# Chunked attention and a token-mixing MLP on one core: q/k in 18-token runs, masked key copies, v by token pairs

## The chip, the cores and the metric

The kernel runs on one core of one Trainium2 chip. The metric is the device time of one execution in microseconds, median of several runs; lower is better. Before the change it is 124.71 us (three runs, 123.63 to 127.87).

## The reference, cut to what matters

```python
# q, k, v: (8, 8, 576, 64) f32: batch, head, token, head dimension
q_c, k_c, v_c = (x.reshape(8, 8, 9, 64, 64) for x in (q, k, v))   # 9 chunks of 64 tokens
scores = q_c @ k_c.transpose(0, 1, 2, 4, 3) / 8.0
attn = softmax(scores, axis=-1)
x = (attn @ v_c).reshape(8, 8, 576, 64).transpose(0, 2, 1, 3).reshape(8, 576, 512)
wq, wk = x @ w_q, x @ w_k                                         # (8, 576, 64)
mixed = (wq @ wk.transpose(0, 2, 1) / 8.0) @ x
out = maximum(mixed, 0) @ w_out                                   # (8, 576, 512) f32
```

Attention stays inside each chunk of 64 tokens, so it is 576 small independent problems. The mixing step has no softmax, so the kernel computes it as wq @ (wk^T @ x) and never forms the 576 x 576 matrix.

## The kernel before, in words

The work goes batch by batch, and every step of every batch is a word in one long list, `ORDER`, which the kernel walks through at the end. A word is a step, a batch, a part and, behind `@`, a PSUM bank; behind `:` stands the engine of a copy, A for ScalarE and D for VectorE. Each engine executes its own instructions strictly in the order of the list. Waits between engines come from the data: an instruction waits until what it reads is written and what it overwrites has been read. So the list sets the order of the work, and the data sets the waits.

The steps of a batch b, with the lines of the profile:

- `LDb.*` (L116, L122, L129): GpSimd issues DMAs that read f32 from DRAM and write f16 into SBUF. q and k go to `qk`, as two runs of 16 tokens per partition and a rest of 4 (`q0-1`, `q1-2`, `qt`; heads 0 to 3 on partitions 0 to 63, heads 4 to 7 on the others). v goes to `vt` token by token, so that one DMA packet carries one token of one head, 256 bytes read and 128 written. There are three `vt` buffers; the load of batch b waits until batch b-3 has been used. All loads share eight completion semaphores in turn, so a load is issued when the load eight places earlier has landed.
- `CLi` (L137, L140): VectorE clears a `vt` buffer once and writes columns of ones. In `vt` two heads stand side by side, one on partitions 0 to 63 and one on 64 to 127, with zeros elsewhere, so that one product handles two heads and the column of ones gives the sum of the exponentials.
- `TRb.x` (L180): VectorE transposes q and k in blocks of 32 x 32, taking two f16 as one f32. Three parts each for q (even x) and k (odd x).
- `SCb.u` (L189): scores on TensorE. Each head uses 32 rows of the array twice (even and odd elements of the head dimension); four heads work side by side. u = 0 and 1 are 64 products of 64 columns each, u = 2 is 16.
- `EXb.u` (L204): the exponential on ScalarE, PSUM to `est`.
- `PVb.u` (L219): attention times v, 12 products each. `RNb.u` (L231, L232): VectorE divides by the sums and writes `xn`.
- `XT`, `XE` (L246, L273 or L275): transpose x through PSUM and copy it back. `PJ`, `EP` (L263): wq and wk. `TL`, `DU`: small copies of them. `WT`, `EW` (L291): transpose wk. `GM`, `EG` (L309): wk^T x, once per batch. `MX`, `RL` (L325, L340, L342): mixed, with the relu. `OM`, `OE` (L362): the output product of 128 rows and its copy out of PSUM, 36 in all; the copies collect in the space of used `qk` tiles, and SyncE stores them (L378).

`WS` loads w_q and w_k from SyncE, `WC` casts them, `WO` loads w_out, `CZ` clears a helper tile `zz` and `wtl`. The first store has a hand-made dependency on the last load, so the stores begin when all loads are done. `copy(eng, ...)` is one helper for all copies, so L273 (ScalarE) and L275 (VectorE) stand for many steps; the profile tells them apart by the tiles.

Of the kernel before, what the change touches and what calls it, by code (L numbers as in the profile page):

```python
# [11 lines left out]
F32 = mybir.dt.float32  # L12
AF = mybir.ActivationFunctionType
# [4 lines left out]
WS LD0.q1-2 CL0 CL1 LD0.q0-1 TR0.0 CZ TR0.2 LD0.k1-2 LD0.k0-1 TR0.3 TR0.1 CL2 LD0.v0-4 LD0.qt LD0.kt LD1.q0-2 ID  # L18
LD1.k0-2 LD1.kt LD1.v0-4 LD1.qt LD2.kt LD2.k0-2 LD2.q0-2 LD2.qt WO LD3.k0-2 LD2.v0-2 LD2.v2-4 SC0.0@0 EX0.0 SC0.1@2
EX0.1 TR0.4 TR0.5 PV0.1@2 RN0.1 PV0.0@0 RN0.0 SC0.2@4 EX0.2 PV0.2@4 TR1.0 RN0.2 TR1.1 TR1.3 TR1.2 TR1.4 TR1.5 XT0.0@0  # L20
XT0.1@4 XE0.1:A WC XE0.0:A SC1.0@2 SC1.1@4 PJ0@0 EX1.0 EX1.1 EP0:A PV1.0@4 SC1.2@2 TL0:A WT0@0 EX1.2 EW0:A PV1.2@2
GM0@0 EG0:A PV1.1@6 LD3.q0-2 LD3.kt LD4.k0-2 LD3.qt LD3.v0-2 LD3.v2-4 LD4.q0-2 LD5.qt LD5.q0-2 LD4.kt LD5.k0-2 LD4.qt
# [5 lines left out]
SC3.1@2 RN3.0 TR4.1 EX3.1 SC3.2@4 GM2@0 EX3.2 EG2:A PV3.1@2 RN3.1 MX2.1@0 RL2.1:A PV3.2@4 MX2.3@6 RL2.3:A MX2.0@0
RL2.0:A XT3.0@2 MX2.2@6 OM6@3 RN3.2 TR4.0 XT3.1@4 SC4.0@0 RL2.2:A XE3.0:D TR5.2 XE3.1:D TR4.5 TR5.1 OM10@2 PJ3@4
LD4.v2-4 LD5.kt LD5.v0-2 LD6.qt LD6.q0-2 LD6.kt LD6.k0-2 LD5.v2-4 LD7.kt LD7.q0-2 LD7.qt LD6.v0-2 LD7.k0-2 LD6.v2-4  # L30
OM11@6 OM7@7 TR4.2 TR4.3 OE10:A EX4.0 EP3:A TR4.4 DU3:D TR5.3 TR5.0 SC4.1@4 PV4.0@0 OE11:A TL3:A OE6:A EX4.1 OE7:A
OM9@3 WT3@2 PV4.1@4 SC4.2@6 OE9:A EW3:A EX4.2 RN4.0 TR5.5 TR5.4 RN4.1 SC5.0@0 EX5.0 PV4.2@6 GM3@2 RN4.2 EG3:A SC5.2@4
EX5.2 MX3.1@2 RL3.1:A MX3.0@0 RL3.0:D MX3.3@4 RL3.3:A XT4.1@6 XT4.0@2 OM12@3 OM13@4 TR6.0 XE4.0:D TR6.5 OE12:D OE13:D
XE4.1:A PJ4@6 OM14@4 MX3.2@2 EP4:A TL4:A RL3.2:A OE14:A TR6.1 TR6.4 TR6.3 PV5.0@6 SC5.1@0 SC6.2@2 EX5.1 OM15@5 WT4@4
EX6.2 EW4:A RN5.0 TR7.5 TR6.2 PV5.1@0 PV5.2@2 GM4@4 RN5.1 RN5.2 DU4:A OE15:A EG4:A OM16@6 MX4.3@4 MX4.1@0 TR7.4
RL4.1:D TR7.2 XT5.0@7 RL4.3:A XE5.0:A OE16:A XT5.1@2 OM17@4 OE17:A SC6.0@0 MX4.0@6 MX4.2@4 RL4.0:A EX6.0 XE5.1:D TR7.0
RL4.2:D TR7.1 PJ5@2 SC7.2@4 SC6.1@6 PV6.0@0 EP5:A LD7.v2-4 LD7.v0-2 OM18@2 TL5:D WT5@3 EX6.1 DU5:A EW5:A EX7.2 RN6.0
PV6.2@6 PV6.1@0 GM5@3 SC7.0@4 EG5:A OE18:D RN6.2 RN6.1 MX5.0@2 EX7.0 RL5.0:A OM20@6 XT6.0@7 MX5.2@4 RL5.2:A MX5.3@2
RL5.3:A MX5.1@0 OE20:D TR7.3 RL5.1:D XE6.0:D OM19@6 SC7.1@4 XT6.1@0 EX7.1 OE19:A XE6.1:D OM24@7 OE24:D PV7.1@4 PV7.0@0
PV7.2@2 PJ6@6 EP6:A RN7.1 RN7.0 RN7.2 TL6:A OM21@4 OM23@5 WT6@0 OM25@1 XT7.0@2 XT7.1@6 OE23:A XE7.0:D EW6:A OE21:A  # L40
XE7.1:D DU6:D GM6@0 EG6:A OE25:A OM22@2 MX6.2@6 MX6.3@0 RL6.3:D RL6.2:A PJ7@4 OM30@3 MX6.1@0 MX6.0@6 EP7:A RL6.1:A
RL6.0:A TL7:D WT7@4 OM26@5 OE22:D EW7:D GM7@4 EG7:A DU7:D OE26:D OE30:A OM29@6 OM28@7 MX7.1@2 RL7.1:D MX7.0@4 RL7.0:A
OE28:A OE29:D OM27@0 OE27:A MX7.3@2 MX7.2@4 RL7.3:D RL7.2:A OM31@1 OE31:A OM32@2 OE32:A OM35@1 OE35:A OM34@2 OE34:A
OM33@1 OE33:A
# [4 lines left out]
def kernel(  # L49
# [23 lines left out]
    RUN = 16  # L73
# [9 lines left out]
    vt = [sb.tile([P, NG, VP], F16, name=f"vt{i}") for i in range(NVB)]  # L83
    qkT = [sb.tile([P, 2, NG * 32, 2], F16, name=f"qkT{i}") for i in range(2)]
# [20 lines left out]
    halves = [x.rearrange("b (f h) s d -> b f (h s) d", f=2) for x in (q, k, v)]  # L105
    lead = NG // 16 * 16 * CH

    def load(b, what):
        s = "qkv".index(what[0])
        part = what[1:]  # L110
        for f in range(2):
            src = halves[s][b, f]
            rows = slice(CH * f, CH * f + CH)
            if s == 2:
                lo, hi = (int(x) * NG // 4 for x in part.split("-"))
                d = nc.gpsimd.dma_start(  # L116
                    vt[b % NVB][rows, lo:hi, f * (D + 2) : f * (D + 2) + D],
                    src.rearrange("(c p) d -> p c d", p=CH)[:, lo:hi, :],
                )
            elif part != "t":  # L120
                lo, hi = (int(x) for x in part.split("-"))
                d = nc.gpsimd.dma_start(  # L122
                    qk[b // 2][rows, b % 2, s, RUN * lo : RUN * hi].rearrange(
                        "p (u r) d -> p u (r d)", r=RUN
                    ),
                    src[0:lead].rearrange("(u p r) d -> p u (r d)", p=CH, r=RUN)[:, lo:hi],
                )
            else:
                d = nc.gpsimd.dma_start(  # L129
                    qk[b // 2][rows, b % 2, s, 32:36].rearrange("p r d -> p (r d)"),  # L130
                    src[lead:].rearrange("(p r) d -> p (r d)", r=4),
                )
            loads.append(d)
# [34 lines left out]
    def tr(b, u, s):  # L168
        at = (slice(0, 16), slice(16, 32), slice(32, 36))[u]
        r = RUN if u < 2 else 4  # L170
        to = qkT[b % 2][:, s].bitcast(F32).rearrange("p n o -> p (n o)")[
            :, 32 * at.start : 32 * at.stop
        ]
        frm = qk[b // 2][:, b % 2, s, at].bitcast(F32)
        if s or u == 2:
            to = to.rearrange("p (x r) -> p r x", r=r)
        else:
            to = to.rearrange("p (c r w) -> p r c w", c=8, r=r)
            frm = frm.rearrange("p r (c w) -> p r c w", c=8)
        nc.vector.transpose(out=to, in_=frm)  # L180

    def sc(b, u, bank):
        for c in range(8 if u < 2 else 2):
            tok = slice(512 * u + CH * c, 512 * u + CH * c + CH)
            for e in range(2):
                for i in range(4):
                    half = CH * (i // 2)
                    rows = slice(32 * i, 32 * i + 32)
                    nc.tensor.matmul(  # L189
                        ps[half : half + CH, bank + i % 2, CH * c : CH * c + CH],  # L190
                        lhsT=qkT[b % 2][rows, 1, tok, e],
                        rhs=qkT[b % 2][rows, 0, tok, e],
                        start=(e == 0),
                        stop=(e == 1),
                    )

    def ex(b, u, bank):
        n = CH * (8 if u < 2 else 2)
        src = ps[:, bank : bank + 2, 0:n]
        dst = est[b % 2][u].rearrange("p i n c -> p i (n c)")  # L200
        if u < 2:
            src = src.rearrange("p i (n r w) -> p (i n) w r", r=RUN, w=CH // RUN)
            dst = dst.rearrange("p i (n w r) -> p (i n) w r", r=RUN, w=CH // RUN)
        nc.scalar.activation(dst, src, AF.Exp, scale=scale_attn)  # L204

# [182 lines left out]
    for word in ORDER:  # L388
# [103 lines left out]
```

## Time and profile before

| What | Value |
|---|---|
| median of the runs | 124.71 us |
| the profiled execution | 124.75 us, span 122.7 us |
| TensorE busy | 94.9 us, 77% of the span |
| VectorE busy | 86.4 us, 70% |
| ScalarE busy | 68.0 us, 55% |
| GpSimd busy (issuing loads) | 64.6 us, 53% |
| DMA packets of the loads' queue | 45,088, 14.69 MB written |
| stores | 16, issued from 94.15 us on |

The span is the time from the first to the last instruction of the profile; the execution's own time is 2.05 us longer. The page gives busy time per engine, a strip of 40 slices (one digit per slice, the busy share in tenths), a chain of waits that ended last, and the costliest groups of instructions. In a line of a group, "out<-in" names the tiles, then come the shapes, the count, the busy time in us, the mean of one in ns, and behind the bar the idle time before them with what ended it. PE is TensorE, DVE VectorE, ACT ScalarE, POOL GpSimd, SP SyncE.

### The profile page before, as it was taken

How to read it: one execution, taken by the hardware profiler on the slowest of the kernel's cores; microseconds unless marked ns; L12 is line 12 of the kernel's file. 1: busy time of each engine (PE TensorE's matmuls, PEld its weight loads, DVE VectorE, ACT ScalarE, POOL GpSimd, SP SyncE). 2: the span in 40 equal slices, each digit the busy share in tenths (PEclk: the TensorE clock that was granted, in tenths of full speed). 3: DMA queues.
4: the chain of work that ended last, by engine and by line, in shares of the span. 5: the costliest groups of instructions: out<-in, count | busy, mean ns of one | idle time of the engine just before them, and what ended most of it. 6: DMA issues, size and time to landing. Idle time of an engine off the chain costs nothing.

```text
span 122.7 us, 4593 instructions
## 1 busy us (share of the span) xinstructions
PE 94.9 (77%) x2000; PEld 60.1 (49%) x2000; DVE 86.4 (70%) x147; ACT 68.0 (55%) x111; POOL 64.6 (53%) x104
## 2 busy tenths in 40 slices
PE   0001476887798899979998889599959999999970
PEld 0001475745573566465655655266536565544320
DVE  5777679624896789789997865799388894763500
ACT  4000610783498736777297936479936725463860
POOL 6997189648864489748985992389300000000000
PEclk9999999999999999999999999999999999999997
DMA  2999999999999999999999999999992999949794
GB/s 32 175 197 160 176 208 164 158 206 162 171 187 162 191 202 156 166 198 205 169 158 118 156 181 175 160 97 161 159 125 39 405 410 405 409 168 407 310 382 174
DMA packets 48499, 24.67 MB, mean 201 GB/s; under 512 B 39776, under 2 KB 42336, under 8 KB 48480
## 3 DMA queue, kind: packets, MB, share of 16 engines
q0 software_dynamic: 45088, 14.69, 113.5%
q1 hardware_dynamic: 3392, 9.70, 20.3%
q8 instruction: 15, 0.25, 0.8%
q14 instruction: 4, 0.03, 0.1%
HBM read 29.62 MB, written 9.44 MB: 318 GB/s over the span
## 4 chain that ended last, share of the span: by engine, by line
PE 42%; DMA 25%; POOL 11%; DVE 7%; issue 7%; ACT 5%; DVEq 0%; ACTq 0%; POOLq 0%
PE pb L362 17%; DMA vt<-in_v_dram 13%; DMA qk<-in_q_dram 6%; DMA qk<-in_k_dram 6%; POOL vt L116 5%; PE pb L263 5%; PE pb L219 5%; POOL qk L122 4%; PE pb L189 4%; DVE qkT L180 4%; PE pb L309 4%; PE pb L246 4%; PE pb L325 2%; DVE xn L232 2%; ACT rmx L340 2%
## 5 line engine op out<-in xcount | busy, mean ns | idle before, releaser
L180 DVE STREAM_TRANSPOSE qkT<-qk 128x512 f32<-128x512 f32 (+1 forms) x48 | 31.4, 706 | 11.6 <-DMA qk<-in_q_dram 6.2
L362 PE MATMUL pb<-wout,rmx 128*128 128x512 f16 x144 | 35.7, 381 | 0.1
L204 ACT ACTIVATE est<-pb 128x1024 f16<-128x1024 f32 (+1 forms) x24 | 19.0, 810 | 17.5 <-PE pb L189 17.5
L116 POOL DMA_DIRECT2D vt<-in_v_dram x28 | 25.3, 919 | 4.3 <-PE pb L189 1.2
L189 PE MATMUL pb<-qkT 32*64 32x64 f16 x1152 | 15.2, 204 | 14.2 <-DVE qkT L180 13.0
L232 DVE TENSOR_TENSOR xn<-pb,rec 128x768 f16<-128x768 f32 x24 | 23.0, 958 | 0.8
L189 PEld LDWEIGHTS <-qkT 32*64 32x64 f16 x1152 | 12.9, 117 | 17.9 <-DVE qkT L180 14.5
L362 PEld LDWEIGHTS <-rmx 128*128 128x128 f16 x144 | 13.0, 103 | 13.9 <-issue 1.6
L340 ACT ACTIVATE rmx<-pb 128x576 f16<-128x576 f32 x24 | 14.9, 651 | 5.4 <-PE pb L325 5.4
L273 ACT COPY qk<-pb 128x512 f32<-128x512 f32 x25 | 14.4, 590 | 5.4 <-PE pb L362 5.2
L219 PE MATMUL pb<-vt,est 128*64 128x130 f16 x288 | 14.2, 247 | 3.8 <-DMA vt<-in_v_dram 2.2
L219 PEld LDWEIGHTS <-est 128*64 128x64 f16 x288 | 11.1, 124 | 5.8 <-ACT est L204 2.4
L122 POOL DMA_DIRECT2D qk<-in_q_dram x18 | 10.5, 593 | 6.4 <-DMA vt<-in_v_dram 4.6
L122 POOL DMA_DIRECT2D qk<-in_k_dram x18 | 10.5, 603 | 5.8 <-DMA vt<-in_v_dram 4.3
L246 PE MATMUL pb<-ident,xn 128*128 128x128 f16 x144 | 11.0, 230 | 2.3 <-DVE xn L232 1.7
L246 PEld LDWEIGHTS <-xn 128*128 128x128 f16 x144 | 9.3, 103 | 4.6 <-issue 1.8
L273 ACT COPY xT<-pb 128x1280 f16<-128x1280 f16 (+1 forms) x6 | 6.9, 1153 | 7.3 <-PE pb L246 7.3
L129 POOL DMA_DIRECT2D qk<-in_q_dram x16 | 8.9, 584 | 3.1 <-DMA qk<-in_k_dram 1.9
L263 PE MATMUL pb<-xT,wpj 128*128 128x512 f16 x64 | 10.1, 305 | 0.4 <-ACT xT L273 0.4
L129 POOL DMA_DIRECT2D qk<-in_k_dram x16 | 8.7, 550 | 2.4 <-DMA qk<-in_k_dram 1.5
L275 DVE COPY qk<-pb 128x512 f32<-128x512 f32 x11 | 7.4, 682 | 1.8 <-PE pb L362 1.7
L275 DVE COPY xT<-pb 128x1024 f16<-128x1024 f16 (+1 forms) x10 | 7.1, 720 | 2.1 <-PE pb L246 2.1
(35 smaller groups left out, 81.1 us busy)
## 6 DMA issues: line engine op xcount, KB each, us to landing
out_dram<-qk SPq DMA_DIRECT2D x10, 768.0 KB, 6.4
qk<-in_q_dram POOLq DMA_DIRECT2D x14, 256.0 KB, 6.5
qk<-in_k_dram POOLq DMA_DIRECT2D x14, 256.0 KB, 6.8
vt<-in_v_dram POOLq DMA_DIRECT2D x24, 144.0 KB, 7.4
out_dram<-qk SPq DMA_DIRECT2D x6, 256.0 KB, 2.4
vt<-in_v_dram POOLq DMA_DIRECT2D x4, 288.0 KB, 7.6
qk<-in_q_dram POOLq DMA_DIRECT2D x4, 128.0 KB, 3.8
qk<-in_k_dram POOLq DMA_DIRECT2D x4, 128.0 KB, 5.3
```

The lines of the kernel that those rows point to most:

```text
L116: d = nc.gpsimd.dma_start(vt[b % NVB][rows, lo:hi, f * (D + 2) : f * (D + 2) + D], src.rearrange("(c p) d -> p c d", p=CH)[:, lo:hi, :],)
L122: d = nc.gpsimd.dma_start(qk[b // 2][rows, b % 2, s, RUN * lo : RUN * hi].rearrange("p (u r) d -> p u (r d)", r=RUN), src[0:lead].rearrang ...
L129: d = nc.gpsimd.dma_start(qk[b // 2][rows, b % 2, s, 32:36].rearrange("p r d -> p (r d)"), src[lead:].rearrange("(p r) d -> p (r d)", r=4),)
L180: nc.vector.transpose(out=to, in_=frm)
L189: nc.tensor.matmul(ps[half : half + CH, bank + i % 2, CH * c : CH * c + CH], lhsT=qkT[b % 2][rows, 1, tok, e], rhs=qkT[b % 2][rows, 0, tok ...
L204: nc.scalar.activation(dst, src, AF.Exp, scale=scale_attn)
L219: nc.tensor.matmul(ps[CH * o : CH * o + CH, bank + m // 3, at : at + VP].rearrange("p (f d) -> p f d", f=2)[:, :, 0 : D + 1], lhsT=est[b % ...
L232: nc.vector.tensor_tensor(out=xn[b % 2][:, 6 * u : 6 * u + 6].rearrange("p (k n) (f d) -> p k (n f) d", k=2, f=2), in0=xv[:, :, :, 0:D], i ...
L246: nc.tensor.transpose(t16[:, at % 1024 : at % 1024 + P], xn[b % 2][:, n, :], ident[:])
L273: nc.scalar.copy(dst, src)
L340: nc.scalar.activation(dst, src, AF.Relu, scale=scale_moe)
L362: nc.tensor.matmul(ps[:, bank, :], lhsT=c.rearrange("p (t r) -> p r t", r=size)[:, r], rhs=wout[:, i, :], start=(i == 0), stop=(i == NI - 1),)
```

## The change

- q and k are loaded as two runs of 18 tokens per partition (`RUN = S // 32`), one DMA for each half (`q0`, `q1`, `k0`, `k1`), all 128 partitions in one DMA. The rest pieces are gone. There are 32 such DMAs for 68.
- `TR` transposes half a batch of q or k at once, 576 elements per partition, two parts for each instead of three. q goes to `qT` (two buffers), k to `kN` (one buffer for all batches).
- New step `MKb.x`: each half of `kN` is copied twice into `kT`, multiplied by a mask that keeps the rows of one of two heads. An engine is named for each of the 32 copies: 18 on VectorE, 14 on ScalarE.
- `SC` takes 64 rows for each product with the two masked copies side by side as 128 columns, so one product gives the scores of two heads: 576 products for 1152. `EX` reads and writes without the rearrangement.
- v is read by pairs of tokens: a packet reads 512 bytes and writes 256, into partitions 32 to 95 only. New step `CPb.x` (`pair`): the second token of each pair is copied on the chip to partitions 0 to 31 or 96 to 127. 28 copies on VectorE, 4 on ScalarE.
- The clears of two `vt` buffers go to ScalarE, as a copy of zeros; the ones come from a small tile.
- `WS` moves behind the first loads, and its transfers wait for the eighth one. `WO` and `WS` are split in two parts each. `ZZ` (a product of zeros with zeros, five times) is new in the list. The first store depends on the second last load, the second on the last.
- `ORDER` is new. By its words, VectorE has 4 `OE` (11 before) and 3 `RL` (8); ScalarE has 32 `OE` (25), 29 `RL` (24) and 9 `XE` (6).

```diff
 ORDER = """
-WS LD0.q1-2 CL0 CL1 LD0.q0-1 TR0.0 CZ TR0.2 LD0.k1-2 LD0.k0-1 TR0.3 TR0.1 CL2 LD0.v0-4 LD0.qt LD0.kt LD1.q0-2 ID
+LD0.k1 MM CZ LD0.q1 LD0.k0 LD0.q0 CL1:D TR0.3 TR0.2 MK0.2:D MK0.3:D TR0.1 MK0.1:D SC0.1@0 TR0.0 MK0.0:D CL0:A LD0.v1
+LD0.v0 LD1.k0 LD1.q1 LD1.v0 LD1.k1 LD1.q0 WS CP0.0:D CP0.2:D CP0.3:D CP0.1:D TR1.1 SC0.2@2 SC0.0@4 CL2:A EX0.1 EX0.0
...
+LD7.v0 LD7.q1 PJ4@0 EP4:A SC5.0@2 OM17@5 OM12@0 SC5.2@6 EX5.0 TL4:A OE13:A OE17:A EX5.2 WT4@1 EW4:A CP5.0:D CP5.1:D
...
     def load(b, what):
+        if what[0] == "v":
+            n = int(what[1:])
+            half = NG // 2
+            for f in range(2):
+                dst = vcols(b % NVB, (2 * D + 2) * f, 2 * D)[
+                    32 + 32 * f : 64 + 32 * f, half * n : half * n + half
+                ]
+                src = v[b, 4 * n + 2 * f : 4 * n + 2 * f + 2].rearrange(
+                    "h (c i e) d -> i (h c) (e d)", i=32, e=2
+                )
+                loads.append(nc.gpsimd.dma_start(dst, src))
+            return
+        s, g = "qk".index(what[0]), int(what[1:])
+        loads.append(
+            nc.gpsimd.dma_start(
+                qk[b // 2][:, b % 2, s, RUN * g : RUN * g + RUN].rearrange("p r d -> p (r d)"),
+                (q, k)[s][b].rearrange("(x g) (p r) d -> g x p (r d)", g=2, r=RUN)[g],
+            )
+        )
+
+    def pair(b, n, f, eng):
+        half = NG // 2
+        g = slice(half * n, half * n + half)
+        to, frm = (slice(0, 32), slice(32, 64)) if f == 0 else (slice(96, P), slice(64, 96))
+        copy(
+            eng,
+            vcols(b % NVB, D + f * (D + 2), D)[to, g],
+            vcols(b % NVB, VW * f, D)[frm, g],
+        )
+
+    def clear(i, eng):
...
+        if eng == "A":
+            nc.scalar.copy(z, zero)
+        else:
+            nc.vector.memset(z, 0.0)
+        copy(eng, one, ones[:, None, :].broadcast_to([P, NG, 2]))
...
+    def tr(b, g, s):
+        to = (kN if s else qT[b % 2])[:, g].bitcast(F32).rearrange("p n o -> p (n o)")
+        frm = qk[b // 2][:, b % 2, s, RUN * g : RUN * g + RUN].bitcast(F32)
+        if s:
+            to = to.rearrange("p (e x r) -> p r e x", e=2, r=RUN // 2)
+            frm = frm.rearrange("p (r e) x -> p r e x", e=2)
         else:
+            to = to.rearrange("p (x r) -> p r x", r=RUN)
         nc.vector.transpose(out=to, in_=frm)
 
+    def mk(b, g, f, eng):
+        dst = kT[b % 2][:, g, :, f].rearrange("p c (e i) o -> p c e (i o)", e=2)
+        frm = kN[:, g].rearrange("p (e c i) o -> p c e (i o)", e=2, c=NCH)
+        if eng == "A":
+            nc.scalar.activation(dst, frm, AF.Copy, scale=mask[:, f : f + 1])
+        else:
+            nc.vector.tensor_scalar(dst, frm, mask[:, f : f + 1], None, op0=ALU.mult)
+
     def sc(b, u, bank):
+        for i in range(8 if u < 2 else 2):
+            g, c = (u, i) if u < 2 else (i, NCH - 1)
             for e in range(2):
+                for t in range(2):
+                    rows = slice(CH * t, CH * t + CH)
                     nc.tensor.matmul(
+                        ps[:, bank + t, CH * i : CH * i + CH],
+                        lhsT=kT[b % 2][rows, g, c, :, :, e].rearrange("p f n -> p (f n)"),
+                        rhs=qT[b % 2][rows, g, CH * c : CH * c + CH, e],
...
-    for d, back in zip(stores, (1,)):
+    for d, back in zip(stores, (2, 1)):
```

More of the change, by code (lines that the diff above doesn't have):

```diff
@@ L17 @@
 ORDER = """
-WS LD0.q1-2 CL0 CL1 LD0.q0-1 TR0.0 CZ TR0.2 LD0.k1-2 LD0.k0-1 TR0.3 TR0.1 CL2 LD0.v0-4 LD0.qt LD0.kt LD1.q0-2 ID
[L19 to L22, printed above, removed]
@@ L28 @@
[L28 to L32, printed above, removed]
@@ L33 @@
[L33 to L42, printed above, removed]
@@ new lines @@
+XE0.1:A WC SC1.0@4 PJ0@6 EX1.0 EP0:A TL0:A ZZ@2 SC1.2@2 EX1.2 WT0@6 EW0:A SC1.1@2 EX1.1 ZZ@0 GM0@0 EG0:A TR2.3 DU0:D
+TR2.1 CP1.3:D CP1.2:D PV1.0@2 MK2.3:A RN1.0 MX0.1@0 MX0.0@6 RL0.1:A RL0.0:A PV1.1@4 RN1.1 MX0.2@0 RL0.2:A MX0.3@2
+RL0.3:A PV1.2@6 MK2.2:A RN1.2 MK2.1:D TR2.2 MK2.0:D TR2.0 XT1.0@4 XE1.0:A OM2@2 CP2.0:D CP2.1:D XT1.1@6 XE1.1:A LD3.v0
+LD3.q1 LD3.v1 LD4.k1 OM0@3 OE0:A SC2.1@4 EX2.1 PJ1@6 LD4.k0 LD4.v0 LD5.k1 LD4.q1 LD4.q0 LD5.q0 LD4.v1 LD5.k0 LD5.q1
+TR3.1 EP1:A SC2.2@0 SC2.0@4 TL1:A EX2.2 EX2.0 DU1:A OE2:A WT1@6 OM1@7 EW1:D MK3.1:D CP2.2:D CP2.3:D MK3.0:D TR3.0
@@ L45 @@
+OM31@3 OE33:A OE31:D OM35@2 OE35:A OM34@0 OE34:A
 """.split()
@@ L72 @@
     VP = 2 * (D + 2)
-    RUN = 16
+    VW = 3 * D + 2
+    RUN = S // 32
     NVB = 3
@@ L82 @@
     qk = [sb.tile([P, 2, 2, NG, D], F16, name=f"qk{i}") for i in range(B // 2)]
-    vt = [sb.tile([P, NG, VP], F16, name=f"vt{i}") for i in range(NVB)]
-    qkT = [sb.tile([P, 2, NG * 32, 2], F16, name=f"qkT{i}") for i in range(2)]
+    vt = [sb.tile([P, (NG + 1) * VW], F16, name=f"vt{i}") for i in range(NVB)]
+    qT = [sb.tile([P, 2, S, 2], F16, name=f"qT{i}") for i in range(2)]
+    kN = sb.tile([P, 2, S, 2], F16, name="kN")
+    kT = [sb.tile([P, 2, NCH, 2, CH, 2], F16, name=f"kT{i}") for i in range(2)]
+    mask = sb.tile([P, 2], F32, name="mask")
+    ones = sb.tile([P, 2], F16, name="ones")
     est = [
@@ L104, with vcols @@
     loads = []
-    halves = [x.rearrange("b (f h) s d -> b f (h s) d", f=2) for x in (q, k, v)]
-    lead = NG // 16 * 16 * CH
+    def vcols(i, at, n):
+        return vt[i][:, at : at + NG * VW].rearrange("p (g c) -> p g c", c=VW)[:, :, 0:n]
     def load(b, what):
[L109 to L118, printed above, removed]
-                )
[L120 to L133, printed above, removed]
@@ L157, in small_weights @@
             for f in range(2):
-                nc.sync.dma_start(
-                    wst[CH * f : CH * f + CH, :, n, :],
-                    w.rearrange("(f k d) j -> f d k j", f=2, d=CH)[f],
+                for t in range(2):
+                    d = nc.sync.dma_start(
+                        wst[CH * f : CH * f + CH, 2 * t : 2 * t + 2, n, :],
+                        w.rearrange("(t f g d) j -> f t d g j", f=2, t=2, d=CH)[f, t],
+                    )
+                tc.add_manual_dep(
+                    d.ins,
+                    loads[7].ins.name,
+                    mybir.DependencyInfo(
+                        mybir.DependencyClass.Sync, mybir.DependencyReason.DATA
+                    ),
                 )
@@ L198, in ex @@
         n = CH * (8 if u < 2 else 2)
[L199 to L204, printed above, removed]
+        nc.scalar.activation(
+            est[b % 2][u].rearrange("p i n c -> p i (n c)"),
+            ps[:, bank : bank + 2, 0:n],
+            AF.Exp,
+            scale=scale_attn,
+        )
     def chunks(n):
@@ L404 @@
         if kind == "CL":
-            clear(n)
+            clear(n, eng or "D")
         elif kind == "CZ":
             nc.vector.memset(zz[:].bitcast(F32), 0.0)
+            nc.vector.memset(ones[:], 0.0)
+            for f in range(2):
+                nc.vector.memset(ones[CH * f : CH * f + CH, f : f + 1], 1.0)
             for w in wtl:
@@ L419 @@
             tr(n, x // 2, x % 2)
+        elif kind == "MK":
+            mk(n, x // 2, x % 2, eng)
+        elif kind == "CP":
+            pair(n, x // 2, x % 2, eng)
+        elif kind == "MM":
+            nc.vector.memset(mask[:], 0.0)
+            for i in range(4):
+                nc.vector.memset(mask[32 * i : 32 * i + 32, i % 2 : i % 2 + 1], 1.0)
         elif kind == "SC":
```

89 lines of the change are left out of this document (44 added, 45 removed).

## The prediction

> **What bounds the kernel now.** I read the engine table first, then the chain that ended last, then the timeline. The page:
>
> ```profile
> PE 94.9 (77%) x2000; PEld 60.1 (49%) x2000; DVE 86.4 (70%) x147; ACT 68.0 (55%) x111; POOL 64.6 (53%) x104
> ACT  4000610783498736777297936479936725463860
> DMA  2999999999999999999999999999992999949794
> ```
>
> TensorE (PE) and VectorE (DVE) are the full engines, ScalarE (ACT) has room, and DMA is busy to the end: loads to about 92 us, then stores. The chain in order of time:
>
> ```profile
> 80.94 7.35 DMA qk<-in_k_dram
> ...
> 88.39 1.04 DVE qkT L180
> ...
> 110.25 0.67 PE pb L309 x12
> ...
> 118.90 0.58 ACT qk L273
> ```
>
> A key load sets the time until 88 us, then TensorE without a gap until 118.9. I use L309 (GM, one per batch) as milestones. By the timeline, GM0 to GM7 end at 31.7, 41.0, 54.7, 68.4, 81.3, 92.5, 105.5 and 110.9 us; 8.6 us later the last compute ends, 3.2 us after that the span (122.7; its execution took 124.75, the median of the runs shown is 124.71). Load waits between GM3 and GM5, by the timeline of DVE (idle time in brackets):
>
> ```profile
> 71.52 0.71 DVE L180 STREAM_TRANSPOSE qkT<-qk 128x512 f32<-128x512 f32 x1 [1.37 <-DMA qk<-in_q_dram]
> 75.63 2.17 DVE L180 STREAM_TRANSPOSE qkT<-qk 128x512 f32<-128x512 f32 x3 [1.40 <-DMA qk<-in_k_dram]
> 79.68 0.93 DVE L180 STREAM_TRANSPOSE qkT<-qk 128x128 f32<-128x128 f32 x2 [0.86 <-DMA qk<-in_k_dram]
> 88.39 1.04 DVE L180 STREAM_TRANSPOSE qkT<-qk 128x512 f32<-128x512 f32 x1 [1.96 <-DMA qk<-in_k_dram]
> ```
>
> Together 5.6 us: that is about all that faster loads can give back there.
>
> **Prices**, from the groups by form:
>
> ```profile
> L204 ACT ACTIVATE est<-pb 128x1024 f16<-128x1024 f32 x16 | 16.2, 1024 | 12.9 <-PE pb L189 12.9
> L340 ACT ACTIVATE rmx<-pb 128x576 f16<-128x576 f32 x24 | 14.9, 651 | 5.4 <-PE pb L325 5.4
> L273 ACT COPY qk<-pb 128x512 f32<-128x512 f32 x25 | 14.4, 590 | 5.4 <-PE pb L362 5.2
> L273 ACT COPY wq<-wqk 64x576 f16<-64x576 f16 x4 | 2.7, 669 | 0.1
> L275 DVE COPY wq<-wqk 64x576 f16<-64x576 f16 x4 | 1.3, 327 | 0.8 <-ACT wqk L273 0.7
> ```
>
> The 64x64 copies (wtl) take 241 ns on ACT and 178 on DVE, so an SBUF element costs 0.84 ns on ACT and 0.29 on DVE. A masked key copy (MK) and a pair move (CP) have 1152 elements a partition: 1.15 us on ACT, 0.49 on DVE.
>
> **The change, part by part.**
>
> *Loads.* Counting the trace's DMA packets: 128-byte v packets pass at 2315 per 2 us (13.8 ns each on 16 engines), the 2048-byte q/k ones at 196 (163 ns). A line through both gives 23.7 ns for a v packet of 256 bytes (estimate; between 20.4 by bytes and 27.6, twice the old one) and 183 for a 2304-byte one. All loads: before 82.8 us, after 77.7 (bounds 74 to 82). POOL issues 68 loads for 98; issuing is hidden behind the packets themselves. The stores start with the second last load instead of the last; the final store follows the last OE in both. The last loads queue behind LD7.v1, which waits for PV4 to release its buffer near 80 us, so they land near 86; TR7.2, which needs the last, comes behind PV6 near 100. So the 5.6 us of waits go. If v packets gain nothing, the last lands near 90, still in time.
>
> *Transposes.* 48 become 32, each 576 elements. The old q form writes runs of four and takes 0.70 us, the k form writes strided and takes 1.04, the 128-element form, strided too, 0.394: 1.68 ns an element. Both new forms are strided: 1.15 us (0.79 if like the fast form, the low end). 36.8 us for 34.1.
>
> *Masked copies and pair moves.* 32 MK (18 on DVE, 14 on ACT) and 32 CP (28 and 4). DVE 46 x 0.49 = 22.5, ACT 18 x 1.15 = 20.7. tensor_scalar with a pointer from SBUF isn't in the trace: on DVE between 0.49 (the copy row) and 1.37 (one element a cycle, as in the fast transpose); I take 0.49, as the operands are f16 as in that row. MK on ACT reads its scale by pointer, which no row shows. The Trainium skill (ScalarE: Activation LUTs, What ACT_TABLE_LOAD costs) gives about 93 ns more for each such operand; by it the sum would be 1.3 us longer.
>
> *Moved to ACT.* Seven more OE (25 to 32, 4.1 us), five RL (24 to 29, 3.3), net three XE (2.8), and two clears: 2 x 2.4 us by the slope, hidden in the start, where ACT waited 10.9 us for its first score; without that cover they cost 4.8. Later DVE drops two clears (4.4), seven OE, five RL. Adding each list, less 0.045 us per instruction (before: ACT rows sum to 73.0, busy 68.0, 111 instructions): ACT 66.8 to 101.2, DVE 88.5 to 98.6.
>
> *Scores.* 1152 products become 576 of twice the width. Old: 64 take 0.64 us in the chain. New 32: between 0.48 (if two row halves run together, as the L325 pairs start together) and 0.96 (L291 transposes, the same 64x128 form, one in 0.030). I take 0.70, no change; the ends are 4 us either way in all. PE 84.2 to 85.5, with five ZZ.
>
> *Start.* By packet prices LD1.q0 lands at 20.6 (16.8 us of loads after a start of 3.8). Then TR1.0, SC1.0, EX1.0 to 23.7, PJ0 at the cold price of 2.08, EP0, WT0, EW0, GM0: end near 28.6 for 31.7 (bounds 27 and 31.7). CP0 waits for v0 (13.1) on DVE with TR1.1 and RN0 queued behind it, so PV0 starts near 15.1 (before 15.5). The weights wait on SP behind the eighth load, land near 18, and WC needs them near 22: covered. Early products are slow: 64 of L189 take 1.07 at 22 us, 0.70 at 35. The Trainium skill (TensorE: Matmul & The Clock Gate, Part 1) says that the clock rises after about 3.4 us of sustained work; the ZZ make that likelier, and by it the start would lose PJ0's 2.08 for 1.14, SC1.0's 1.07 for 0.70 and GM0's 1.32 for 0.74, 1.9 us. As TensorE is idle between these groups, I take none.
>
> *Sum.* I cut both order lists at the GM and add the prices, PE/DVE/ACT. Before: 7.3/8.9/7.3, 11.6/13.3/9.0, 12.4/13.2/10.3, 9.6/9.2/6.8, 9.2/8.3/8.7, 12.8/12.3/7.0, 5.5/1.8/3.3; the largest of each add to 72.5, measured 79.2, less 5.6 of load waits 73.6: a factor of 1.02. After: 9.2/15.1/11.9, 11.8/9.8/14.7, 9.2/14.4/12.7, 9.7/9.5/11.8, 11.0/9.9/11.6, 12.7/13.6/12.2, 6.5/3.0/5.4: 87.7 by stage, 81.4 by two stages (DVE and ACT lead in turn and may run ahead). Middle 84.5, times 1.02 is 86.2. So GM7 ends at 28.6 + 86.2 = 114.8, plus 8.6 and 3.2: span 126.6, plus 2.05: **128.6 us**. ACT, at 80% of its span, is the new bound. One more wait: kN is a single buffer, so a key transpose waits for the two MK before it, some on the full ACT queue, with RN and CP queued behind on DVE; I leave it in the factor.
>
> **Rivals.**
>
> *A, ScalarE packs (faster).* In a full ACT queue neighbours overlap more: two OE take 1.08 for 1.18, two RL 1.19 for 1.30, some 0.10 each. If ACT always has the next operand ready, its 80.3 us from GM0 to GM7 shrink by 97 x 0.055 to 75: GM7 at 103.6 to 107 with up to 4% of gaps, us 117.5 to 121. It decides once ACT's gaps stay below 4%. For it: bursts of three RL (1.74). Against: of 111 old instructions most didn't pack, and DVE, with 75 us there, must keep pace.
>
> *B, a swap.* The two-stage bound holds without the factor (81.4): us 123.8. For it: start and waits give 3.1 and 5.6 back. Against: between GM0 and GM3 the old stages took their largest sum or a little more.
>
> *C, no fast mode in the 46 DVE moves:* 0.88 more each, 40 us on DVE: about 160. Against: the 0.327 row.
>
> *D, the v part doesn't do what it says:* a packet of twice the bytes takes twice as long (27.6 ns), so CP is pure cost. Three v halves are ahead of LD1.q0, 1152 packets and 0.28 us each, so the start is 0.8 later: 129.4. Against: 4 KB packets pass more bytes per ns than short ones. The Trainium skill (DMA: Bandwidth & Descriptors, Specifications) puts full rate at transfers of 512 bytes and up, which the new writes of 256 still miss; that speaks for D.
>
> **How the numbers follow.** Forecast 0.46 (own range 125.5 to 133), A 0.24, B 0.19, C 0.05, D 0.06. Faster by over 2% (under 122.2; 2% is about what a measurement of this kernel can tell from no change): A and a little of B, 0.27. Within: most of B and the forecast's edge, 0.20. Slower (over 127.2): 0.53. The range leaves out the end of A, C and the tail: 119 to 137.
>
> **What would show it.** Right: ACT busy near 100 us, DVE 95 to 100, no DMA wait of L206 transposes past 30 us, GM0 near 28.6, GM stages with ACT or DVE full. Wrong: transposes near 0.8, MK or CP on DVE near 1.3, ACT below 90, or PE waits on loads past 60 us.

## The result, and the profile after

The changed kernel takes 142.46 us (median) against 125.13 for the kernel before in the same comparison: ratio 1.133, 95% interval 1.101 to 1.165, clearly slower. The forecast was 128.6, its range 119 to 137. Some executions of one and the same kernel are longer than its others by one to four per cent; the ratio, and every difference in time below, leaves them out, and then the changed kernel takes 140.7 us (140.00 and 141.36) and the kernel before 124.2. The profiled execution took 140.0 us with a span of 138.2.

The page of the changed kernel: the engine table, then strips of 40 slices of 3.5 us each.

```profile
PE 96.2 (70%) x1429; PEld 58.3 (42%) x1429; DVE 99.7 (72%) x160; ACT 101.2 (73%) x151; POOL 47.5 (34%) x74
...
ACT  7900033384459999999999798599999999786640
...
GB/s 13 44 160 182 175 153 123 141 161 144 126 137 163 163 151 163 169 152 132 176 137 135 147 174 154 166 184 153 163 103 236 265 418 411 405 143 153 290 274 199
```

The engines hold the work that was forecast (VectorE 99.7 us for 98.6, ScalarE 101.2 for 101.2), and yet the span is 11.6 us longer than the forecast span of 126.6. ScalarE's strip hints where: it is full only from the thirteenth slice on, at 41 us. The milestones (end of GM, L344 now) by the timeline:

| | GM0 | GM0 to GM7 | GM7 to the end of the span | span |
|---|---|---|---|---|
| before | 31.7 | 79.2 | 11.8 | 122.7 |
| forecast | 28.6 | 86.2 | 11.8 | 126.6 |
| after | 42.2 | 84.9 | 11.1 | 138.2 |

The start holds the whole miss: GM0 ends 13.6 us later than forecast. Its timeline, first VectorE, then ScalarE (idle time and what ended it in brackets):

```profile
12.60 1.20 DVE L206 STREAM_TRANSPOSE kN<-qk 128x576 f32<-128x576 f32 x1 [7.72 <-DMA qk<-in_k_dram]
```

```profile
36.25 0.62 ACT L194 CAST wpj<-rmx 128x512 f16<-128x512 f32 x1 [3.49 <-DMA rmx<-in_moe_w_k_dram]
```

and the chain that ended last, in order of time:

```profile
6.49 12.29 DMA vt<-in_v_dram
22.69 13.46 DMA rmx<-in_moe_w_k_dram
36.92 2.12 PE pb L298 x8
```

The first key load was issued at 1.26 us and its transpose began at 12.60. The small weights, held behind the eighth load, were issued from 18.8 us on, the last piece of w_k at about 22.7, and landed at 36.15. The cast WC stands on ScalarE ahead of EX1.0, and PJ0 on TensorE waits for it. "Land near 18" was wrong by 18 us, and with it "covered". Every load is slow, not the first alone (DMA issues: count, KB, median us to landing; before, q and k took 6.5 and 6.8):

```profile
qk<-in_k_dram POOLq DMA_DIRECT2D x16, 288.0 KB, 11.1
qk<-in_q_dram POOLq DMA_DIRECT2D x16, 288.0 KB, 10.9
vt<-in_v_dram POOLq DMA_DIRECT2D x32, 144.0 KB, 10.8
```

The packets tell why. The row of the loads' queue (packets, MB, their time as a share of 16 engines' span):

```profile
q0 software_dynamic: 36416, 14.73, 113.4%
```

Of these packets the trace counts 13,376 of 4 bytes, before 1,568. Before, that is 16 for each of 98 loads. After, 68 loads x 16 = 1,088 leave 12,288, which is 384 for each of the 32 q/k loads. A q/k load has 128 data packets. If four engines carry them, each has 32, and 12 idle engines with as many 4-byte packets each make 12 x 32 = 384. From 5 us on the 2304-byte packets landed per us climb 19, 34, 44, 68, 87 as loads are added; four engines at 183 ns pass 22, sixteen pass 87. The trace does not name the engine of a packet, but both counts fit a q/k load that runs on 4 of 16 (theory T1). What changed is the shape of its read: `"(x g) (p r) d -> g x p (r d)"` takes every second head, four stretches of 32 runs with a gap between, so the slowest dimension counts 4. In the kernel before it counted 64. The Trainium skill (DMA: Bandwidth & Descriptors, Why a DMA increments its semaphore by 16 and not by 1) states this rule: the largest number up to 16 that divides the slowest dimension of both sides is the number of engines. The counts agree. I priced the packets and did not look at the outer dimension.

Rival theories: T2, the weights' new place in the queue is the cause by itself; T3, the added copies on VectorE and ScalarE are.

### The profile page after: what moved, and what is told of

Its sections match the earlier page's. It is cut to its first block, busy times and chain, and to the rows that moved or that the text cites. A ratio compares the mean times of both kernels' runs of the same rounds, so it can differ in the third digit from the quotient of the medians.

```text
span 138.2 us, 3452 instructions
## 1 busy us (share of the span) xinstructions
PE 96.2 (70%) x1429; PEld 58.3 (42%) x1429; DVE 99.7 (72%) x160; ACT 101.2 (73%) x151; POOL 47.5 (34%) x74
## 4 chain that ended last, share of the span: by engine, by line
DMA 36%; PE 27%; ACT 20%; DVE 6%; issue 3%; SPq 3%; POOL 1%; ACTq 0%; DVEq 0%
DMA vt<-in_v_dram 16%; PE pb L397 12%; DMA qk<-in_q_dram 10%; DMA rmx<-in_moe_w_k_dram 10%; ACT est L232 5%; PE pb L298 4%; PE pb L281 4%; DVE xn L267 4%; ACT rmx L375 3%; PE pb L222 3%; ACT qk L308 3%; SPq L181 3%; ACT kT L212 2%; PE pb L360 2%; DVE qT L206 2%
## 5 line engine op out<-in xcount | busy, mean ns | idle before, releaser
L222 PE MATMUL pb<-qT,kT 64*128 64x64 f16 x576 | 13.5, 200 | 22.7 <-DVE kT L214 18.2
L129 POOL DMA_DIRECT2D vt<-in_v_dram x32 | 21.6, 677 | 20.3 <-DMA qk<-in_q_dram 5.7
L206 DVE STREAM_TRANSPOSE kN<-qk 128x576 f32<-128x576 f32 x16 | 19.4, 1215 | 11.5 <-DMA qk<-in_k_dram 11.3
L222 PEld LDWEIGHTS <-kT 64*128 64x128 f16 x576 | 11.4, 101 | 28.6 <-DVE kT L214 18.3
L206 DVE STREAM_TRANSPOSE qT<-qk 128x576 f32<-128x576 f32 x16 | 19.6, 1242 | 4.6 <-DMA qk<-in_q_dram 4.6
L212 ACT ACTIVATE kT<-kN,mask 128x1152 f16<-128x1152 f16 x14 | 17.5, 1265 | 3.0 <-DVE rec L264 2.8
L133 POOL DMA_DIRECT2D qk<-in_q_dram x16 | 11.7, 731 | 13.1 <-DMA vt<-in_v_dram 6.1
L133 POOL DMA_DIRECT2D qk<-in_k_dram x16 | 11.3, 707 | 12.1 <-DMA qk<-in_k_dram 6.6
L310 DVE COPY vt<-vt 32x1152 f16<-32x1152 f16 x28 | 12.4, 458 | 1.0 <-DMA vt<-in_v_dram 0.3
L360 PE MATMUL pb<-wqk,g 64*128 64x288 f16 x32 | 7.1, 290 | 5.3 <-DVE xn L267 2.3
L308 ACT COPY xT<-pb 128x1024 f16<-128x1024 f16 (+1 forms) x9 | 9.6, 1095 | 0.0
(44 smaller groups left out, 95.3 us busy)
## 6 DMA issues: line engine op xcount, KB each, us to landing
qk<-in_k_dram POOLq DMA_DIRECT2D x16, 288.0 KB, 11.1
```

What stands on the lines that cost most here:

```text
L129: loads.append(nc.gpsimd.dma_start(dst, src))
L133: nc.gpsimd.dma_start(qk[b // 2][:, b % 2, s, RUN * g : RUN * g + RUN].rearrange("p r d -> p (r d)"), (q, k)[s][b].rearrange("(x g) (p r) ...
L212: nc.scalar.activation(dst, frm, AF.Copy, scale=mask[:, f : f + 1])
L222: nc.tensor.matmul(ps[:, bank + t, CH * i : CH * i + CH], lhsT=kT[b % 2][rows, g, c, :, :, e].rearrange("p f n -> p (f n)"), rhs=qT[b % 2] ...
L308: nc.scalar.copy(dst, src)
```

## The experiments

**One stretch per q/k load (e1_all_engines).** The heads are dealt out so that a load reads four neighbouring heads; v then needs one load per head, and the weight rows follow. With more v loads, the load that the small weights wait for is the twelfth and no longer the eighth; it is the same one, the last of `LD0.v0`.

```diff
-                (q, k)[s][b].rearrange("(x g) (p r) d -> g x p (r d)", g=2, r=RUN)[g],
+                (q, k)[s][b].rearrange("(g x) (p r) d -> g (x p) (r d)", g=2, r=RUN)[g],
...
-                src = v[b, 4 * n + 2 * f : 4 * n + 2 * f + 2].rearrange(
-                    "h (c i e) d -> i (h c) (e d)", i=32, e=2
-                )
+                for h in range(2):
+                    src = v[b, 4 * h + 2 * n + f].rearrange("(c i e) d -> i c (e d)", i=32, e=2)
...
-                        moe_w_out.rearrange("(t f g p) m -> f t p g m", f=2, t=2, p=CH)[f, t],
+                        moe_w_out.rearrange("(g t f p) m -> f t p g m", f=2, t=2, p=CH)[f, t],
...
-                    loads[7].ins.name,
+                    loads[11].ins.name,
```

> The changed kernel with its head order altered: partition quarter x of half g holds head 4g + x instead of 2x + g, so that a q/k load reads one unbroken stretch of 128 runs and not four stretches of 32; v is then loaded per head (64 loads of v instead of 32) and the weight rows follow. Bytes, packets (128 of 2304 B for each q/k load) and all compute stay. T1 (the four stretches of a q/k load put it on 4 of the 16 DMA engines, so its 128 packets take 32 x 183 ns = 5.9 us in a row instead of 8 x 183 ns = 1.5 us): the first load lands at about 6.5 to 8 us and not 12.5, w_k lands by 28 and not 36, the first GM ends at 28 to 32 and not 42.2, and the time is 42.2 - 30 = 12 us less, 125 to 131 us; the 4-byte packets of the q/k queue fall from 13,376 to some 1,600. T2 (the small weights, issued only behind the eighth load, set the start by themselves): the first GM ends at 38 or later and the time is 136 or more. T3 (the added masked copies on VectorE and ScalarE set the start): the first GM ends within 3 us of 42.2, time 137 to 142.

126.92 us, ratio to the kernel before 1.017 (1.005 to 1.028): 14.0 us less than the changed kernel (126.7 for 140.7). The 4-byte packets are 1,600 = 100 loads x 16. The row of the loads' queue, VectorE's first transpose, and the strip of GB/s:

```profile
q0 software_dynamic: 24640, 14.69, 84.8%
```

```profile
5.39 1.22 DVE L208 STREAM_TRANSPOSE kN<-qk 128x576 f32<-128x576 f32 x1 [0.51 <-DMA qk<-in_k_dram]
```

```profile
GB/s 24 183 197 172 188 187 207 192 189 181 187 145 196 168 160 175 189 203 193 173 137 131 204 188 210 183 115 122 302 410 408 404 191 204 134 5 245 257 318 188
```

The first transpose starts at 5.39 for 12.60; the second slice moves 183 GB/s for 44. GM0 ends at 33.4 (forecast of T1: 28 to 32, missed by 1.4), GM0 to GM7 takes 81.1 us for 84.9. T1 holds; T3 can have little of it. w_k still lands at 26.3 and the cast still waits 3.0 us.

**v per head alone (e10_v_per_head_only)**, the control for the other half of that edit.

```diff
-                src = v[b, 4 * n + 2 * f : 4 * n + 2 * f + 2].rearrange(
-                    "h (c i e) d -> i (h c) (e d)", i=32, e=2
-                )
+                for h in range(2):
+                    src = v[b, 4 * n + 2 * f + h].rearrange("(c i e) d -> i c (e d)", i=32, e=2)
...
-                    loads[7].ins.name,
+                    loads[11].ins.name,
```

> Control for the one-stretch run, which changed the v loads as well: the changed kernel with v loaded per head (64 loads of 72 KB instead of 32 of 144 KB), its q/k loads left in four stretches. T1 (the q/k pattern alone made the difference): no gain; 32 x 0.6 us more for issues on GpSimd and the same q/k loads: 140 to 148 us, first GM at 41 to 44. T7 (smaller v loads, which free the window of loads in flight sooner, are part of the gain): first GM at 39 or earlier, 130 to 138 us.

162.99 us: not a gain but 19 us more (159.5 for 140.7), beyond what I expected of T1 too. VectorE's waits (us in total, times, longest):

```profile
DVE kN L208 <- DMA qk<-in_k_dram: 20.3, 8, 7.0
DVE qT L208 <- DMA qk<-in_q_dram: 17.8, 7, 4.7
```

So the v split alone brings no gain; with it in both runs the q/k pattern is worth 33 us, 159.5 to 126.7. What the split does to one-stretch loads no run shows, so the 14.0 us are the worth of both halves of the edit together. My reading is that eight loads are in flight at most, and four-engine loads need four of their kind among them to fill 16 engines; twice as many v loads leave fewer places. That is argued from the window of eight, not shown by a run.

**The weights first (e2_weights_first).** `WS` at the head of the list, without the dependency on the eighth load.

```diff
-LD0.k1 MM CZ LD0.q1 LD0.k0 LD0.q0 CL1:D ...
-LD0.v0 LD1.k0 LD1.q1 LD1.v0 LD1.k1 LD1.q0 WS CP0.0:D ...
+WS LD0.k1 MM CZ LD0.q1 LD0.k0 LD0.q0 CL1:D ...
+LD0.v0 LD1.k0 LD1.q1 LD1.v0 LD1.k1 LD1.q0 CP0.0:D ...
...
-                tc.add_manual_dep(d.ins, loads[7].ins.name, ...)
```

> The changed kernel with the small weights w_q and w_k issued first of all and without their wait for the eighth load; nothing else is changed. T1 (the q/k loads on 4 engines set the start; the weights are only one of the things that they delay): the cast of the weights no longer waits 3.5 us and the projection no longer 3.3 us, the first GM ends at about 39 and the time falls by some 3 us, to 136 to 140. T2 (the late weights are the whole loss): the first GM ends at 32 or earlier, time 127 to 132. T3 (the copies): first GM within 1.5 us of 42.2, time 140 to 143.

140.62 us. GM0 ends at 38.9 (for 42.2), as T1 said, and T2 falls. How much of the 3.3 us reaches the end stays open: three executions took 140.6 to 140.9 us and one took 137.8, which is 2.9 less than the changed kernel. In the profiled one, of 140.58 us, GM0 to GM7 takes 89.0 us for 84.9. VectorE's waits for loads in it:

```profile
DVE kN L199 <- DMA qk<-in_k_dram: 13.7, 7, 7.4
DVE qT L199 <- DMA qk<-in_q_dram: 5.7, 4, 2.8
DVE vt L303 <- DMA vt<-in_v_dram: 2.2, 3, 0.8
```

These are 21.6 us, in the changed kernel 16.2: in this execution what the weights give back is waited for later.

**Both (e3_engines_and_weights)**, the diffs of the one-stretch run and of the weights together.

> Both edits together: the changed kernel with the q/k loads in one stretch of 128 runs each, and the small weights issued first. T1 (the start was lost to loads on 4 engines, and behind them to the weights that queue after the eighth load): the cast of the weights and the projection behind it, which in the run with the one-stretch loads still waited 3.0 us for w_k landing at 26.3, wait for nothing; the first GM ends at 29 to 30.5 instead of 33.4, the rest stays (81 us to the last GM, 10.7 us behind it), so a span of 121 to 122.5 and a time of 122.5 to 124.5 us: 0 to 2% under the kernel before. T3 (the copies on VectorE and ScalarE are what is left of the start): first GM at 32 or later, time 126 or more.

125.22 us over 12 runs, ratio 0.998 (0.9935 to 1.0029): level with the kernel before. GM0 ends at 30.7; both figures lie just above T1's ranges (30.5 and 124.5), and below what T3 asked for. The weights are worth 1.5 us here (126.7 to 125.2). The two edits, one of layout and one of order, take back the whole loss: the ratio of 1.133 becomes 0.998.

**The engine count in another kernel.** The kernel before with its 16-token loads issued one unit at a time (control), and the same with the 64 runs of a load read as 4, 8 or 16 stretches. Only the pattern's order differs; the tokens come out permuted.

```diff
-                    src[0:lead].rearrange("(u p r) d -> p u (r d)", p=CH, r=RUN)[:, lo:hi],
+                    src[0:lead].rearrange("(u c a r) d -> u a c (r d)", c=CH // 4, a=4, r=RUN)[u],
```

> Control for the run with four stretches: the kernel before, with each q/k load issued per 16-token unit in two loads instead of one, its 64 runs read in their own order. All theories: within 2.5% of the kernel before (123 to 128 us); some 0.5 to 1 us more for the additional issues at the start, and 4-byte packets at 16 for each load.

> The kernel before, with each q/k load issued per 16-token unit and its 64 runs read as 4 stretches of 16 with a step between (the tails of 4 tokens likewise); the tokens land on other partitions, so the output is that of permuted tokens. Bytes, packets and compute are those of the kernel before. T1 (outermost count of 4 puts a load on 4 engines): packets of 4 B on the load queue rise from 1,568 by some 300 for each such load, the first loads take 16 packets in a row on each engine instead of 4 (some 2 us longer each), the first GM ends 4 to 12 us later than in its control, and the time is 130 to 140 us. T2 and T3 (it is the weights, or the copies, that cost the changed kernel its start; the pattern of the read does nothing): like its control within 1.5%, 123 to 127 us.

> The kernel before with the 64 runs of a q/k load read as 16 stretches of 4 with a step between (tails likewise; the output is that of permuted tokens). It tells the engine count from the broken order of the read. T1 (the number of engines is set by the outermost count, here 16): like the control, 131 to 134 us, some 2,000 packets of 4 B, first GM at 32 to 33. T4 (a read in stretches is slow in itself, whatever their number): like the run with four stretches, 145 or more.

> The same with 8 stretches of 8 runs. T1 (8 engines of 16): 8 packets in a row on each engine, 8 idle engines with as many 4-byte packets each, so 2,016 + 96 x 64 = 8,160 of them, and a time between the control's 132.6 and the four stretches' 154.5, nearer to the control since two loads in flight fill all engines: 134 to 143. T4: 145 or more.

| slowest dimension | time, us | ratio to before (interval) | 4-byte packets | first GM ends |
|---|---|---|---|---|
| 64 (control) | 132.61 | 1.062 (1.039 to 1.084) | 2,016 | 32.4 |
| 16 | 130.98 | 1.038 (1.030 to 1.047) | 2,016 | 32.7 |
| 8 | 136.5 | 1.083 (1.069 to 1.096) | 8,160 | 34.1 |
| 4 | 154.47 | 1.238 (1.222 to 1.254) | 20,448 | 38.5 |

The count of 8,160 is the expected one; for four, 126 loads x 16 + 96 loads x 12 engines x 16 packets = 20,448. Sixteen stretches cost nothing, so it is not the broken order of the read but the count of its slowest dimension. Four cost 22 us over the control, more than I expected (130 to 140 us in all); eight lie 2% over it with intervals that overlap, so there only the packets speak. The control itself missed its expectation: 28 more issues cost 6%, some 8 us and not 1, and no run shows why. With four stretches VectorE waits 36.5 us for q/k loads, in the control 14.3.

**Without most masked copies (e7_no_masked_copies).** On top of both edits, `MK` only for batches 0 and 1.

```diff
         elif kind == "MK":
-            mk(n, x // 2, x % 2, eng)
+            if n < 2:
+                mk(n, x // 2, x % 2, eng)
```

> The run with both edits, and the 48 masked key copies (MK) of batches 2 to 7 left out: their scores read the masked keys of batches 0 and 1, so the output of those batches is that of other keys. It takes 48 of 64 copies, about 27 x 0.5 us off VectorE and 14 x 1.27 us off ScalarE, and the wait of the scores for them. T5 (behind the start the kernel stands at the 85 to 100 us of VectorE and ScalarE work, and the masked copies are what eats the gain of the halved score products): the 81 us from the first to the last GM fall by 8 to 15 us, time 108 to 116. T6 (the stages are set by TensorE and the loads; the copies lie beside them): less than 4 us, time 119 to 124.

The counts in that text are off: there are 32 copies, and 24 are left out, 12 on each engine (VectorE busy 94.9 for 100.5, ScalarE 88.8 for 100.6). 122.7 us, ratio 0.965 (0.953 to 0.977): 3.5 us less than with the copies (121.7 for 125.2), 78.0 us from GM0 to GM7 for 81.2. This is T6's range: 17 us of work less on the two fullest engines gives 3.2 in the middle. Stages of the run with both edits (start:end, length, then busy us of PE, PEld, DVE, ACT, POOL, the granted clock, DMA share, GB/s):

```profile
31.00:42.00 11.00, 9.87 (x172) 6.14 (x168) 10.04 (x17) 10.89 (x16) 6.98 (x12) 1.00 1.39 178
42.00:56.50 14.50, 12.79 (x209) 7.86 (x211) 14.13 (x22) 14.39 (x22) 10.55 (x18) 1.00 1.18 163
```

ScalarE is full, VectorE at 91 and 97%, TensorE at 90 and 88%: three engines within 12%. My reading is that emptying one or two hands the bound to the next: without the copies TensorE and VectorE are at 90 to 93% of the same two stages (9.83 and 9.86 of 10.6 us, 12.57 and 12.88 of 14.0).

**Copies balanced (e8_copies_balanced).** Seven `MK` from ScalarE to VectorE, four `XE` the other way, on top of both edits.

```diff
-... MK2.3:A MK3.2:A MK4.2:A MK4.1:A MK5.3:A MK6.1:A MK7.2:A ... XE2.0:D XE3.1:D XE4.0:D XE5.1:D
+... MK2.3:D MK3.2:D MK4.2:D MK4.1:D MK5.3:D MK6.1:D MK7.2:D ... XE2.0:A XE3.1:A XE4.0:A XE5.1:A
```

> The run with both edits, seven masked key copies moved from ScalarE (1.27 us each) to VectorE (0.53), and four of the evictions XE moved the other way (0.68 to 0.82 us on VectorE, 1.03 to 1.23 on ScalarE). ScalarE then has 7 x 1.27 - 4.7 = 4.2 us less, VectorE 7 x 0.53 - 3.1 = 0.6 us more. T5 (behind the start ScalarE is the bound: it is busy 11.0, 14.4, 12.1, 11.3 and 11.6 us of five stages of 11.0, 14.5, 12.2, 11.4 and 11.7 in the run with both edits): the 81.2 us from the first to the last GM fall by 1.5 to 3.5 us, time 121.5 to 124, faster than the kernel before. T6 (VectorE, at 11.1 of 11.4, or the order of the program binds as much): within 1 us of the run with both edits, 124 to 126.

134.42 us (131.7 to 136.3) where the run with both edits takes 125.2, on less work (ScalarE busy 97.8 us for 100.6, VectorE 100.9 for 100.5): T5 falls, and T6 did not expect this either. In the profiled execution, of 134.79 us, GM1 to GM2 takes 19.9 us for 14.6. TensorE's timeline there, and the stage behind it:

```profile
52.09 0.66 PE L217 MATMUL pb<-qT,kT 64*128 64x64 f16 x32 [1.69 <-DVE kT L209]
54.08 2.08 PE L293 MATMUL pb<-xT,wpj 128*128 128x512 f16 x8 [1.34 <-ACT xT L303]
```

```profile
54.00:58.00 4.00, 3.92 (x30) 1.84 (x30) 0.57 (x2) 3.18 (x8) 2.39 (x5) 0.50 1.12 204
```

SC3.1 waits for the moved key copies, PJ2 for the moved XE; then the granted clock is 0.50 from 54 to 58 us and PJ2 takes 2.08 us for 1.14.

**Five MK moved, nothing moved back (e9_masked_copies_on_vector).**

```diff
-... MK3.2:A ... MK4.1:A ... MK5.3:A ... MK6.1:A ... MK7.2:A
+... MK3.2:D ... MK4.1:D ... MK5.3:D ... MK6.1:D ... MK7.2:D
```

> The run with both edits, with five masked key copies of the middle batches (3.2, 4.1, 5.3, 6.1, 7.2) moved from ScalarE to VectorE and no eviction moved back. ScalarE has 5 x 1.27 = 6.3 us less, VectorE 5 x 0.53 = 2.6 us more, in the 81 us from the first to the last GM. T5 (ScalarE's work is the bound of the middle stages, and what made the balanced run slow was only the evictions XE, which on ScalarE came late for TensorE): 1 to 3 us under the run with both edits, 122 to 124.5 us. T6 (VectorE binds as much): equal or up to 2 us more, 125 to 127.

130.62 us, ratio 1.062 (1.044 to 1.080), 5 us over the run with both edits: both theories missed. The same place again:

```profile
52.57 0.66 PE L217 MATMUL pb<-qT,kT 64*128 64x64 f16 x32 [2.22 <-DVE kT L209]
```

```profile
54.00:58.00 4.00, 4.00 (x45) 2.03 (x44) 1.94 (x3) 3.37 (x8) 3.54 (x6) 0.61 1.21 200
```

The idle time alone does not decide it. Later in the same execution TensorE stands idle for longer, and the clock stays at 1.00 in this stretch and in the next:

```profile
69.19 0.78 PE L217 MATMUL pb<-qT,kT 64*128 64x64 f16 x40 [2.59 <-DVE kT L209]
```

```profile
66.00:70.00 4.00, 1.41 (x74) 1.24 (x74) 3.85 (x8) 1.38 (x3) 4.00 (x8) 1.00 1.11 147
```

**The gaps filled (e12_balanced_filled).** The balanced run with dummy products in TensorE's three idle stretches.

```diff
-... TR4.3 SC3.1@2 EX3.1 PJ2@0 ... XE5.1:A PJ5@4
+... TR4.3 ZZ@2 ZZ@2 SC3.1@2 EX3.1 ZZ@6 ZZ@6 PJ2@0 ... XE5.1:A ZZ@6 ZZ@6 ZZ@6 PJ5@4
```

> The run with the balanced copies, with seven dummy products (zeros, 0.6 us each, into a bank that is free) put on TensorE where it stood idle for 1.7, 1.3 and 2.4 us ahead of SC3.1, PJ2 and PJ5. No wait is taken away. T8 (part of that run's loss is the granted clock, which fell to 0.50 at 54 to 58 us and below 1 again at 95 to 99, right behind those idle stretches): the clock stays at 1.0 there, a projection after the first gap takes 1.1 us again and not 2.1, and the time falls by 3 to 6 us, to 128 to 131. T9 (the idle time itself is the whole loss; the clock is a side effect that other waits hide): within 1.5 us of 134.4.

131.81 us, just short of what T8 asked for (131 at most), and outside T9's range as well. T8's mechanism is there:

```profile
53.99 1.14 PE L293 MATMUL pb<-xT,wpj 128*128 128x512 f16 x8 [0.80 <-ACT xT L303]
```

```profile
54.00:58.00 4.00, 3.97 (x52) 2.20 (x52) 1.94 (x4) 3.94 (x8) 2.97 (x5) 1.00 1.11 201
```

What the clock costs is told by the executions of the unfilled list. One of the six had a mean granted clock of 1.00 and took 131.70 us, as long as the filled run; the five with 0.957 to 0.987 took 133.8 to 136.3. So the falls of the clock go with 2 to 4.6 us. With the filling one of four executions fell below 0.99, without it five of six, which is little to go by. The other 6.5 us, from 125.2 to 131.7, come without a fall of the clock; the waits shown above are the likely cause: the list was made for its own assignment of engines, and a copy moved to a cheaper engine can stand later in that engine's queue. No version here that does all the work is faster than the kernel before.

## Why the prediction was wrong, point by point

- **The packet prices stood; the number of engines under them did not.** In the fullest 2 us 1,239 v packets of 256 bytes landed, 25.8 ns each on 16 engines with some q/k packets among them; in the run with one-stretch loads 1,361, or 23.5 ns (forecast 23.7). That rules out rival D's 27.6. In that run 175 q/k packets landed per 2 us, the 183 ns of the forecast. "LD1.q0 lands at 20.6" and "after 77.7" divided by 16 engines, which a four-engine load fills only with three more of its kind in flight. LD1.q0 was transposed at 31.2, after a wait of 1.5 us for it. This is the step that failed.
- **"The weights ... covered"** failed with it: they hung on the eighth load and landed at 36.15 for 18. Moved first they bring GM0 3.3 us forward in the changed kernel, and 1.5 us of the time with the loads on all engines.
- **"So the 5.6 us of waits go"** held for its own stage: between GM3 and GM5 VectorE waits for no load. But other waits came: 16.2 us in all (11.5 before), 7.7 of them at the first load and 3.4 between GM2 and GM3. With both edits it is 4.2, and none behind GM0.
- **The middle came out near (84.9 for 86.2) by two errors that cancel.** With the loads on all engines it is 81.1 to 81.2: rival B's two-stage sum of 81.4, without the factor of 1.02. The changed kernel adds load waits, and one stage behind them with a granted clock of 0.88 (81.2 to 95.3 us). With both edits the profiled execution took 124.36, where B said 123.8; that nearness is in part luck, as GM0 ends 2.1 us later than B took it and the part behind GM7 is 1.1 us shorter. B's sum for the middle fits, in a kernel whose loads do what I assumed.
- **Instruction prices stood**, by the groups of the changed kernel:

```profile
L206 DVE STREAM_TRANSPOSE kN<-qk 128x576 f32<-128x576 f32 x16 | 19.4, 1215 | 11.5 <-DMA qk<-in_k_dram 11.3
L206 DVE STREAM_TRANSPOSE qT<-qk 128x576 f32<-128x576 f32 x16 | 19.6, 1242 | 4.6 <-DMA qk<-in_q_dram 4.6
L214 DVE TENSOR_SCALAR kT<-kN,mask 128x1152 f16<-128x1152 f16 x18 | 9.5, 548 | 0.1
L212 ACT ACTIVATE kT<-kN,mask 128x1152 f16<-128x1152 f16 x14 | 17.5, 1265 | 3.0 <-DVE rec L264 2.8
L310 DVE COPY vt<-vt 32x1152 f16<-32x1152 f16 x28 | 12.4, 458 | 1.0 <-DMA vt<-in_v_dram 0.3
```

  Transposes take 1.22 and 1.24 us (1.15 forecast), masked copies on VectorE 0.55 and pair moves 0.46 (0.49 each), so C is out. 32 of the new score products take 0.67 us (0.70). A masked copy on ScalarE takes 1.265, the pair move of the same size 1.15: the 0.11 us between them fit the scale by pointer, which the sum left out. The Trainium skill (ScalarE: Activation LUTs, What ACT_TABLE_LOAD costs) gives about 93 ns for it, near the measured 0.11 us. The two clears on ScalarE took 2.16 us each; the slope gives 2.14 for their 2,340 elements, not the 2.4 of the working, and nothing hung on it.
- **A** is out: with both edits ScalarE is busy for about 99% of five stages, and GM0 to GM7 still takes 81.2 us, not A's 75 to 78. That ScalarE's busy time met the forecast 101.2 to a tenth is luck: the working starts from 66.8 us where the kernel before has 68.0, a gap of the size of its one table load (1.28 us), and gave the masked copies 1.6 us too little.

## What to carry to other kernels

Before pricing a DMA by its packets, read the slowest dimension of both its patterns: a count of 4 put these loads on 4 of 16 engines, by the packets, and cost 14 us here and 22 in the kernel before (154.5 for 132.6), while sixteen stretches cost nothing. A quick sign in the trace is the number of 4-byte packets: 16 for each load went with 16 or more in the slowest dimension, 80 with 8, and 208 or 400 with 4. And when three engines are within a tenth of each other in a stage, take work away before moving it: both tries here to move copies within a tuned list came late for TensorE and cost 5 us or more.

## What the hardware showed that I had not expected

- The 4-byte packets beyond 16 for each load fit one rule: each unused engine has as many as a used one has data packets (384 for 128 data packets on 4 engines, 192 for 64 on 4, 64 for 64 on 8). The trace does not name the engine of a packet, so which engine carries them is inferred.
- A stretch of 2.2 us without work on TensorE, and in another run two of 1.7 and 1.3 us with 0.66 us of work between, were followed by 4 us at a granted clock of 0.61 and 0.50. A stretch of 2.59 us in the first of these runs was not, so the length of one stretch does not decide; what does is not shown here. With 0.6 us pieces of work in the gaps the clock was 1.00 in the profiled execution. The Trainium skill (TensorE: Matmul & The Clock Gate, Part 1) speaks of an idle window of about 3.4 us; in front of these two falls no single idle stretch was that long.
- Splitting loads without changing a byte cost some 8 us in the kernel before (28 issues more) and 19 us in the changed one (32 more); the cause of neither is shown.
